# Tile 1's attention heads moved to the plain float32 path, and the weight decodes spread anew

## The chip, the cores and the metric

The kernel runs on one core of one Trainium2 chip. The metric is the device time of one execution in microseconds (us). Three executions of the kernel before gave 879.23, 880.64 and 881.67 us; the median is 880.64 us.

## The reference

Three stages, all in float32 (the four MLP weights of the second and third stage arrive as float64):

```python
# attention: batch 4, 8 heads, 576 positions, head size 64, causal window of 128, ALiBi slopes
scores = (q @ k.T) / 8 - slope[h] * |i - j|          # only where 0 <= i - j < 128
attn = softmax(scores);  x = attn @ v                # x: 2304 tokens x 512
# first MLP: 512 -> 2048 -> 512
x = (s * relu(x @ w_in) ** 2 + b) @ w_out
# second MLP: 512 -> 1024 -> 1024 -> 512
out = (((x @ w1) * (x @ w2)) @ w3) @ w_out2
```

## The kernel before

The 2304 tokens are six tiles of 384. A tile has eight heads in three query blocks of 128; heads are numbered through, g = 8 * tile + head, so tile 0 has g 0 to 7 and tile 1 has g 8 to 15. A query block sees two key blocks of 128, its own and the one ahead of it.

Attention exists in two forms. The **split path** (tiles 1 to 5) cuts each operand into a rounded float32r part and a float32r rest, so that TensorE runs one fast pass per product. Per head: `att_split_q`, `att_split_k` (ScalarE, VectorE, GpSimd), scores in six float32r matmuls (L302, L303, tile `s`), `att_min` on VectorE (L316, L325: both key halves are folded into one of 128 columns, since a query sees at most 128 keys), exp on ScalarE (L339), the division by the sum (`att_norm`, GpSimd L352), three transposes on TensorE (L371, `tp`), a rounded part and a rest (L383, L384, `pp`), two selections on GpSimd that unfold the halves again (L387, `pt`), eight matmuls with V (L424, `pv`), and an addition (L455, L456). The **plain path** (tile 0, `g < EARLY`) does scores in three float32 matmuls on the raw operands (L297), folds nothing, exponentiates 256 columns a block (L333), transposes each key half by itself (L364, `te`), copies (L378, L379, `oe`), multiplies with V that has a column of ones beside it (L404, `xo`), and divides at the end by the sum that this column gave (L436 to L441, `xs`); three more transposes for each pair of heads (L446, `xt`) turn the result.

The first MLP runs 16 chunks for each tile: `mlp_h` (L485 in tile 0, in plain float32; L494 in the others, float32r in three passes) and `mlp_x` (L540, L546, `acc`). Its weights are decoded from float64 beforehand, 32 pieces, each with one operation on ScalarE (L102) and three on VectorE (L104, L107, L113). `tick()` starts one decode and moves those under way by a step.

The order of work: `slot(n, m)` handles one head and, with m, two MLP chunks. Eight slots do tile 0's heads alone; then `"BBBABBABBB"` runs tile 0's MLP in eight slots (B) with the heads 8 to 17 beside it, two of them alone (A); then each slot has a head and two chunks of tiles 1 and up. A scheduler orders the instructions of each engine from a simulated timeline. `tick` is called 1 or 2 times in the head slots (12 in all) and 3 times in each B slot. PSUM has two pools of four banks: `ps_acc`, and `ps_rot` in turn for `s` (two tiles a head), `tp` or `te`, `pv` and `hp`. ScalarE takes its instructions strictly in the order given.

Of the kernel before, what the change touches and what calls it, by code (L numbers as in the profile page):

```python
# [21 lines left out]
P = 128  # L22
TT = 384
# [9 lines left out]
EARLY = H  # L33
# [7 lines left out]
def kernel(  # L41
# [172 lines left out]
    qkraw, vraw, qa, ka, kb, vv, ns, pr, mins, sums, tps, pt, xf, xT, xo = ({} for _ in range(15))  # L214

    def att_load(g):
        if g < NG:
            if g < EARLY and g % 2:
                return
            n = 2 * TT + P + (1 if g < EARLY else 0)  # L220
            raw = ap.tile([P, n], F32, tag="qkraw", name="qkraw", bufs=2)
            nc.sync.dma_start(out=raw, in_=qk0[g // 2] if g < EARLY else qk[g - EARLY])
            if g < EARLY:
                qkraw[g + 1] = raw
            qkraw[g] = raw

    def att_load_v(g):
        if g < NG and g % 2 == 0:
            m = 2 * (D + 1) if g < EARLY else 2 * D
            raw = ap.tile([P, NB + 1, m], F32, tag="vraw", name="vraw", bufs=2)  # L230
            src = v0[g // 2] if g < EARLY else v[(g - EARLY) // 2]
            nc.sync.dma_start(out=raw.rearrange("p n d -> p (n d)"), in_=src)
            vraw[g // 2] = raw

    def att_split_q(g):
        if g < NG:
            sc = -0.125 * 2.0 ** (g % H + 1)
            q_r = qkraw[g][:, :TT]
            if g < EARLY:
                if g % 2 == 0:  # L240
                    a = ap.tile([P, TT], F32, tag="qa", name="qe", bufs=2)
                    nc.scalar.activation(
                        out=a, in_=q_r, func=AF.Identity, scale=qkraw[g][:, -1:]
                    )
                    qa[g] = qa[g + 1] = a
                return
# [8 lines left out]
    def att_split_k(g):  # L255
        if g < NG:
            k_r = qkraw.pop(g)[:, TT:2 * TT + P]
            if g < EARLY:
                ka[g] = k_r
                return  # L260
# [8 lines left out]
    def att_split_v(g):  # L269
# [3 lines left out]
        if g < EARLY:  # L273
# [12 lines left out]
    def att_scores(g):  # L286
# [4 lines left out]
        if g < EARLY:  # L291
            keep_active(s0.rearrange("p n q -> p (n q)"), 2 if g else 10)
        for i in range(NB):
            qs, ks = slice(i * P, (i + 1) * P), slice(i * P, (i + 2) * P)
            if g < EARLY:
                hs, c0 = slice(g % 2 * D, (g % 2 + 1) * D), P if i == 0 else 0
# [9 lines left out]
    def att_min(g):  # L306
        t, h = divmod(g, H)
        dst = ns.pop(g)
        odd = g < EARLY and g % 2
        n = ap.tile([P, NB, 2 * P], F32, tag="vv" if odd else "ns", name="ns")  # L310
        mn = ep.tile([P, NB], F32, tag="mn", name="mn")
        if g >= EARLY:
            e = ap.tile([P, NB, P], F32, tag="pr", name="pr", bufs=2)
        for i in range(NB):
            cs = slice(P if g < EARLY and i == 0 else 0, None)
# [6 lines left out]
        if g < EARLY:  # L322
# [5 lines left out]
    def att_exp(g):  # L328
        e, mn = pr[g], mins.pop(g)
        if g < EARLY:  # L330
            for i in range(NB):
                cs = slice(0 if i else P, None)
# [12 lines left out]
    def att_norm(g):  # L345
        if g < EARLY:
            return
# [9 lines left out]
    def att_transpose(g):  # L357
        e = pr.pop(g)
        if g < EARLY:
# [14 lines left out]
    def att_select(g):  # L374
        tp = tps.pop(g)
        if g < EARLY:
            o = ap.tile([P, 2 * NB, P], F32, tag="pt" if g % 2 else "pp", name="oe")
            nc.scalar.activation(out=o[:, 1:4], in_=tp[0][:, 1:], func=AF.Copy)  # L378
# [14 lines left out]
    def att_v(g):  # L393
        t = g // H
        p, e = divmod(g, 2)
        if g < EARLY:
            o = pt.pop(g)
            if e == 0:
                xo[p] = ps_acc.tile([P, NB, 2, D + 1], F32, tag="acc", name="xo")
            x = vv[p].rearrange("p n (e d) -> p n e d", e=2)  # L400
            for i in range(NB):
                for half in range(2):
                    if i or half:
                        nc.tensor.matmul(  # L404
                            out=xo[p][:, i, e, :], lhsT=o[:, 2 * i + half, :],
                            rhs=x[:, i + half, e, :], start=(half == 0 or i == 0),
# [22 lines left out]
    def att_x(g):  # L429
        t, h = divmod(g, H)  # L430
        p, e = divmod(g, 2)
        if g < EARLY:
            if e:
                acc = xo.pop(p)
                rs = ep.tile([P, NB, 2, 1], F32, tag="sm", name="rs")
# [4 lines left out]
                xs = ap.tile([P, NB, 2, D], F32, tag="cs", name="xs")  # L440
                nc.vector.tensor_tensor(  # L441
                    out=xs, in0=acc[:, :, :, :D], in1=rs.to_broadcast([P, NB, 2, D]), op=ALU.mult
                )
                xf[p] = ps_acc.tile([P, TT], F32, tag="acc", name="xt")
# [13 lines left out]
    def att_xt(g):  # L458
        if g % 2:
            t, h = divmod(g, H)  # L460
            f = xf.pop(g // 2)
            if g < EARLY:
# [499 lines left out]
    def slot(n, m, extra=None):  # L962
# [8 lines left out]
        dec = 2 if mlp and q < NC1 else 1  # L971
# [3 lines left out]
        if s1:  # L975
            splits(n)
            att_scores(n)
            if n + 1 != EARLY:
# [24 lines left out]
        elif n < EARLY:  # L1003
            tick(1 + n % 2)
# [28 lines left out]
        if att:  # L1033
            att_load(n + (2 if n + 2 >= EARLY else 3))
# [4 lines left out]
    for n in range(EARLY):  # L1039
        slot(n, None)  # L1040
    flush(EARLY - 1)
    n, m = EARLY, 0
# [154 lines left out]
```

## Time and profile before

| | |
|---|---|
| median of three runs | 880.64 us |
| the profiled execution, its own time | 882.35 us |
| its span, first to last instruction | 880.6 us |
| TensorE (PE) busy | 857.8 us, 97% of the span |
| VectorE (DVE) busy | 563.5 us, 64% |
| ScalarE (ACT) busy | 485.8 us, 55% |
| GpSimd (POOL) busy | 388.6 us, 44% |
| DMA | 129.57 MB, mean 147 GB/s |

Three stretches matter here: tile 0's heads until 42.27 us, tile 0's MLP with the heads 8 to 16 from there to 143.45 us, and the change to tile 1's MLP until about 164 us. In the timeline each row gives the start, the duration, the engine, the line, the operation, the tile written and those read, and the number of records; a float32 matmul of the program stands as two records. The difference between the starts of two rows is the time that TensorE took for the first of them.

### The profile page before, as it was taken

The numbers are of one execution on the slowest core, as the hardware profiler recorded it, in microseconds if no ns is written. First come the engines' busy times: TensorE is split into PE (matmuls) and PEld (weight loads), VectorE is DVE, ScalarE is ACT, GpSimd is POOL, SyncE is SP. The second block draws the span as 40 slices with busy tenths as digits, with TensorE's granted clock in tenths as the row PEclk, the third lists the DMA queues.
The fourth block names the chain that finished last, engine by engine and source line by source line (L and its number), as shares of the span: only waits on it lengthen the run. The fifth ranks groups of instructions, "written<-read, shape, count | busy, mean of one in ns | idle before, by whom it ended". The sixth has DMA issues, their size and how long they took to land. (4 is left out here: it accounts for less than half of the span.)

```text
span 880.6 us, 13686 instructions
## 1 busy us (share of the span) xinstructions
PE 857.8 (97%) x4676; PEld 777.2 (88%) x4676; DVE 563.5 (64%) x1167; ACT 485.8 (55%) x1140; POOL 388.6 (44%) x419
## 2 busy tenths in 40 slices
PE   8999998999999999999999999999999999999998
PEld 5666666999999999999999999889898889989996
DVE  6888898666878798778863998355434344334233
ACT  6666556777776787777764766344322333222222
POOL 0157666777667676667752302544321233101110
PEclk9999999999999999999999999999999999999999
DMA  8854522112344546445422577824508452530001
GB/s 333 331 200 135 203 84 65 59 55 79 105 147 159 168 168 197 152 168 169 149 96 97 170 260 272 312 84 144 179 28 296 144 183 96 206 117 1 1 1 73
DMA packets 51478, 129.57 MB, mean 147 GB/s; under 512 B 5968, under 2 KB 21328, under 8 KB 51408
## 3 DMA queue, kind: packets, MB, share of 16 engines
q1 hardware_dynamic: 51408, 128.69, 42.6%
q8 instruction: 37, 0.61, 0.3%
q14 instruction: 33, 0.27, 0.1%
HBM read 96.16 MB, written 32.51 MB: 146 GB/s over the span
## 5 line engine op out<-in xcount | busy, mean ns | idle before, releaser
L494 PE MATMUL hp<-x,w 128*128 128x384 f32 x960 | 186.9, 341 | 2.7 <-DVE pp L384 2.5
L494 PEld LDWEIGHTS hp<-x,w 128*128 128x128 f32 x960 | 168.2, 189 | 3.4 <-DVE pp L384 2.7
L546 PE MATMUL acc<-gh,w 128*128 128x384 f32 x640 | 126.3, 339 | 0.8 <-ACT gh L515 0.7
L546 PEld LDWEIGHTS acc<-gh,w 128*128 128x128 f32 x640 | 109.0, 188 | 1.6 <-ACT gh L515 1.4
L815 PE MATMUL d<-xb,wblk 128*128 128x384 f32 x576 | 107.9, 335 | 0.0
L815 PEld LDWEIGHTS d<-xb,wblk 128*128 128x128 f32 x576 | 101.2, 188 | 2.0
L352 POOL TENSOR_SCALAR pr<-pr,sm 128x128 f32<-128x128 f32 x120 | 64.5, 552 | 83.0 <-DVE sm L350 22.7
L913 POOL TENSOR_TENSOR p<-mc 128x384 f32<-128x384 f32 (+2 forms) x30 | 31.3, 1050 | 146.3 <-DVE mc L908 143.9
L815 PE MATMUL u<-xb,wblk 128*128 128x384 f32 x432 | 84.3, 337 | 4.0 <-ACT mc L823 4.0
L387 POOL TENSOR_SCALAR_AFFINE_SELECT pt<-pp 128x768 fp32r<-128x768 f32 x80 | 77.2, 985 | 17.8 <-DVE pp L384 7.9
L854 PE MATMUL oacc<-w3o,ph 128*128 128x512 f32 x270 | 84.8, 395 | 0.0
L815 PEld LDWEIGHTS u<-xb,wblk 128*128 128x128 f32 x432 | 75.2, 188 | 6.8 <-ACT mc L823 6.6
L264 POOL TENSOR_TENSOR kb<-qkraw,ka 128x512 fp32r<-128x512 f32 x40 | 56.6, 1414 | 54.4 <-ACT ka L263 53.9
L904 DVE TENSOR_TENSOR mc<-d,mc 128x384 f32<-128x384 f32 x24 | 13.4, 557 | 94.4 <-PE d L815 94.4
L546 PE MATMUL acc<-gl,w 128*128 128x384 f32 x320 | 69.8, 338 | 2.9 <-DVE gl L523 2.9
L316 DVE CUSTOM_DVE_ANT_0 ns<-s,relm_sb 128x256 f32<-128x256 f32 (+1 forms) x144 | 52.7, 413 | 28.0 <-PE s L303 21.7
L339 ACT ACTIVATE pr<-pr,mn 128x128 f32<-128x128 f32 x120 | 46.9, 392 | 28.0 <-DVE pr L325 27.8
L523 DVE TENSOR_TENSOR gl<-r,gh 128x384 fp32r<-128x384 f32 x80 | 54.2, 678 | 10.4 <-ACT gh L515 9.2
L546 PEld LDWEIGHTS acc<-gl,w 128*128 128x128 f32 x320 | 56.4, 188 | 4.0 <-DVE gl L523 3.9
L854 PEld LDWEIGHTS oacc<-w3o,ph 128*128 128x128 f32 x270 | 50.4, 188 | 10.4
L505 ACT ACTIVATE r<-hp 128x384 f32<-128x384 f32 x96 | 46.4, 484 | 22.1 <-PE hp L494 16.3
L606 POOL TENSOR_TENSOR xs<-xs,xh 128x384 fp32r<-128x384 f32 x28 | 30.1, 1091 | 64.3 <-ACT xh L605 39.4
(120 smaller groups left out, 1683.2 us busy)
## 6 DMA issues: line engine op xcount, KB each, us to landing
qkraw<-qk SPq DMA_DIRECT2D x41, 448.0 KB, 3.3
late<-st SPq DMA_DIRECT2D x23, 512.0 KB, 3.3
w<-late SPq DMA_DIRECT2D x23, 512.0 KB, 6.0
raw<-w_in SPq DMA_DIRECT2D x16, 512.0 KB, 6.1
raw<-w_out SPq DMA_DIRECT2D x16, 512.0 KB, 6.6
wr<-w SPq DMA_DIRECT2D x16, 512.0 KB, 4.7
st<-w3T SPq DMA_DIRECT2D x15, 512.0 KB, 3.7
xs<-x2d SPq DMA_DIRECT2D x32, 192.0 KB, 2.9
```

What stands on the lines that cost most here:

```text
L264: nc.gpsimd.tensor_tensor(out=kl, in0=k_r, in1=k.bitcast(F32), op=ALU.subtract)
L316: nc.vector.tensor_tensor_reduce(out=n[:, i, cs], in0=dst[i][:, cs], in1=relm_sb[:, VARIANT.get(t * NB + i, 0), cs], scale=2.0 ** -(h + 1) ...
L339: nc.scalar.activation(out=e[:, i, :], in_=e[:, i, :], func=AF.Exp, scale=-1.0, bias=mn[:, i:i + 1], accum_out=sm[:, i:i + 1],)
L352: nc.gpsimd.tensor_scalar(out=e[:, i, :], in0=e[:, i, :], scalar1=sm[:, i:i + 1], scalar2=1.0, op0=ALU.mult, op1=ALU.mult,)
L387: nc.gpsimd.affine_select(out=o[:, :, :, e, :], in_=pp.bitcast(F32), pattern=[[0, 2], [0, NB], [sign, P]], compare_op=op, fill=0.0, base=0 ...
L494: nc.tensor.matmul(out=hp, lhsT=wi[c][:, l, k * P:(k + 1) * P], rhs=xT[t, k][:, r, :], start=(n == 0), stop=(n == 3 * KD - 1),)
L505: nc.scalar.activation(out=rt[:, :TT], in_=hps.pop((t, c)), func=AF.Relu)
L523: nc.vector.tensor_tensor(out=gl, in0=rt[:, :TT], in1=gh.bitcast(F32), op=ALU.subtract)
L546: nc.tensor.matmul(out=x2acc[m], lhsT=wo[c][:, l, ms], rhs=g[r], start=(c == 0 and n == 0), stop=(c == NC1 - 1 and n == 2),)
L815: tc.keep_in_program_order(nc.tensor.matmul(out=dst, lhsT=w[:, l, ks], rhs=xblk[bnm, k][:, r, :], start=(start and n == 0), stop=(n == 5), ...
L854: tc.keep_in_program_order(nc.tensor.matmul(out=oacc[t, i], lhsT=p[l][:, cs], rhs=w3o[c][:, r, :], start=(c == 0 and n == 0), stop=(c == N ...
L913: nc.gpsimd.tensor_tensor(out=x, in0=u2[:, n:n + w], in1=m5[:, n:n + w], op=ALU.mult)
```

## The change

`EARLY = H` becomes `PLAIN = 2 * H`: heads 8 to 15 take the plain path too. Places that hold for tile 0 alone now ask `g < H`: the missing first key block, the filling matmuls (`keep_active`), and the pool of `xo` and `xt`. In tile 1 `xo` is a bank of `ps_rot` for each head, `xt` one for each pair, and the rest of the turned result is subtracted on VectorE instead of GpSimd. `tick` now runs once in each head slot (8) and four times in each B slot. q, k and V of tile 1 arrive by pairs of heads, as tile 0's do; the load of head 8 that was issued twice is issued once.

```diff
-EARLY = H
+PLAIN = 2 * H
@@ att_scores
-        if g < EARLY:
+        if g < H:
             keep_active(s0.rearrange("p n q -> p (n q)"), 2 if g else 10)
...
-            if g < EARLY:
-                hs, c0 = slice(g % 2 * D, (g % 2 + 1) * D), P if i == 0 else 0
+            if g < PLAIN:
+                hs, c0 = slice(g % 2 * D, (g % 2 + 1) * D), P if g < H and i == 0 else 0
@@ att_transpose
-                for b in range(max(b0, 1), b0 + n):
+                for b in range(max(b0, int(g < H)), b0 + n):
@@ att_v
-            if e == 0:
+            if g >= H:
+                xo[p] = ps_rot.tile([P, NB, 1, D + 1], F32, tag="rot", name="xo")
+            elif e == 0:
                 xo[p] = ps_acc.tile([P, NB, 2, D + 1], F32, tag="acc", name="xo")
@@ att_x
-                xf[p] = ps_acc.tile([P, TT], F32, tag="acc", name="xt")
+            if e:
+                pool, tag = (ps_acc, "acc") if g < H else (ps_rot, "rot")
+                xf[p] = pool.tile([P, TT], F32, tag=tag, name="xt")
@@ att_xt
-                nc.gpsimd.tensor_tensor(
+                (nc.vector if g < PLAIN else nc.gpsimd).tensor_tensor(
                     out=y[:, 1, :], in0=f, in1=y[:, 0, :].bitcast(F32), op=ALU.subtract
@@ slot
-        dec = 2 if mlp and q < NC1 else 1
+        dec = 3 if mlp and q < NC1 else 1
...
-        elif n < EARLY:
-            tick(1 + n % 2)
+        elif n < H:
+            tick(1)
...
-            att_load(n + (2 if n + 2 >= EARLY else 3))
+            if n + 2 >= PLAIN:
+                att_load(n + 2)
+            elif n % 2 and n + 3 < PLAIN:
+                att_load(n + 3)
```

ScalarE at the end of tile 0's heads, before: the exponentials of heads 6 and 7 are L333, the copies of transposed blocks L378 and L379, a decode's first step L102, the preparation of head 8's operands L248 and L263.

```order
L333 ACTIVATE ns<-ns,mn 128x256
L333 ACTIVATE ns<-ns,mn 128x128
L333 ACTIVATE ns<-ns,mn 128x256
L378 ACTIVATE oe<-te 128x384
L379 ACTIVATE oe<-te 128x256
L102 ACTIVATE z<-raw 128x512
L378 ACTIVATE oe<-te 128x384
L333 ACTIVATE ns<-ns,mn 128x256
L248 ACTIVATE qa<-qkraw 128x384
L263 ACTIVATE ka<-qkraw 128x512
```

The same place now (the copies are L379 and L380):

```order
L333 ACTIVATE ns<-ns,mn 128x128
L333 ACTIVATE ns<-ns,mn 128x256 x2
L333 ACTIVATE ns<-ns,mn 128x128
L333 ACTIVATE ns<-ns,mn 128x256 x2
L379 ACTIVATE oe<-te 128x384
L380 ACTIVATE oe<-te 128x256
L379 ACTIVATE oe<-te 128x384
L380 ACTIVATE oe<-te 128x256
L242 ACTIVATE qe<-qkraw 128x384
```

The decode and the copies that stood between head 7's exponentials now stand elsewhere, and the six exponentials follow one another.

TensorE in the middle of tile 0's MLP, before: a slot with one head (L302, L303 scores, L371 transposes, L424 the product with V) and four chunk steps of `mlp_h` (L485) and `mlp_x` (L540).

```order
L302 MATMUL s_1330<-ka,qa 128x256
L303 MATMUL s_1330<-kb,qa 128x256
L302 MATMUL s_1331<-ka,qa 128x256
L303 MATMUL s_1331<-kb,qa 128x256
L540 MATMUL acc<-r,wz 128x386 x4
L371 MATMUL tp<-ident,pr 128x128 x3
L485 MATMUL hp<-xe,wz 128x384 x4
L424 MATMUL pv<-pt,vv 128x256 x2
L424 MATMUL pv<-pt,vv 128x128 x2
L424 MATMUL pv<-pt,vv 128x256 x2
L424 MATMUL pv<-pt,vv 128x128 x2
L540 MATMUL acc<-r,wz 128x386 x4
```

Such a slot now (L297 scores, L364 transposes, L407 the product with V, L455 the turning of a pair; `mlp_h` is L494 and `mlp_x` L549):

```order
L297 MATMUL s_861<-qkraw,qe 128x256 x2
L297 MATMUL s_862<-qkraw,qe 128x256
L364 MATMUL te<-ident,ns 128x128 x6
L549 MATMUL acc<-r,wz 128x386 x4
L494 MATMUL hp<-xe,wz 128x384 x4
L407 MATMUL xo<-vraw,oe 128x65 x6
L494 MATMUL hp<-xe,wz 128x384 x4
```

Three float32 score matmuls stand where six float32r ones stood, six transposes where three stood, and six products with V where eight stood; the chunk steps around them are the same in number.

## Rows read from the trace of the kernel before

**Rows 1.** Busy time (us), share and instructions of TensorE over the span.

```profile
PE 857.8 (97%) x4676; PEld 777.2 (88%) x4676; DVE 563.5 (64%) x1167; ACT 485.8 (55%) x1140; POOL 388.6 (44%) x419
```

**Rows 2.** Busy time of each engine by stretch, then granted clock, DMA share, GB/s.

```profile
42.27:143.45 101.18, 97.88 (x400) 64.12 (x400) 87.49 (x196) 60.88 (x157) 62.63 (x70) 1.00 0.42 142
164.11:480.00 315.89, 313.66 (x1957) 311.67 (x1957) 237.71 (x499) 229.54 (x568) 213.10 (x242) 1.00 0.40 132
```

**Rows 3.** Timeline of TensorE in tile 0's heads (start, us, line, tile, records).

```profile
13.78 0.77 PE L364 MATMUL te<-ident,ns 128*128 128x128 f32 x5
14.38 0.59 PE L78 MATMUL s<-zeros 128*128 128x512 bf16 x2
...
27.15 1.35 PE L297 MATMUL s<-qkraw,qe 64*128 64x128 f32 x6
28.43 0.77 PE L364 MATMUL te<-ident,ns 128*128 128x128 f32 x5
29.16 0.55 PE L446 MATMUL xt<-ident,xs 128*128 128x128 f32 x3
29.54 1.23 PE L404 MATMUL xo<-vraw,oe 128*128 128x65 f32 x10
30.61 0.59 PE L78 MATMUL s<-zeros 128*128 128x512 bf16 x2
31.13 0.92 PE L297 MATMUL s<-qkraw,qe 64*128 64x128 f32 x4
```

**Rows 4.** Timeline of TensorE in tile 0's MLP, with the split heads.

```profile
53.77 4.68 PE L485 MATMUL hp<-xe,wz 128*128 128x384 f32 x14
58.28 2.76 PE L540 MATMUL acc<-r,wz 128*128 128x386 f32 x8
...
90.42 0.57 PE L302 MATMUL s<-ka,qa 128*128 128x256 f32 x1
90.83 0.28 PE L303 MATMUL s<-kb,qa 128*128 128x256 f32 x1
90.95 0.28 PE L302 MATMUL s<-ka,qa 128*128 128x256 f32 x1
...
100.14 0.58 PE L302 MATMUL s<-ka,qa 128*128 128x256 f32 x1
```

**Rows 5.** Timeline of TensorE, rows with a wait ahead of them (in brackets).

```profile
36.55 0.69 PE L364 MATMUL te<-ident,ns 128*128 128x128 f32 x2 [1.64 <-ACT ns L333]
...
106.35 2.85 PE L485 MATMUL hp<-xe,wz 128*128 128x384 f32 x8 [1.23 <-DVE mn L316]
...
137.54 2.85 PE L485 MATMUL hp<-xe,wz 128*128 128x384 f32 x8 [0.79 <-ACT r L505]
...
155.16 3.49 PE L494 MATMUL hp<-x,w 128*128 128x384 f32 x12 [2.52 <-DVE pp L384]
```

**Rows 6.** Timeline of ScalarE ahead of the wait at 36.55.

```profile
35.05 0.66 ACT L102 ACTIVATE z<-raw 128x512 f32<-128x512 f32 x1
...
35.97 0.52 ACT L333 ACTIVATE ns<-ns,mn 128x256 f32<-128x256 f32 x1
```

**Rows 7.** Stretches of 2 us, columns as in rows 2.

```profile
36.00:38.00 2.00, 1.46 (x4) 1.15 (x5) 1.94 (x5) 1.70 (x5) 0.50 (x1) 0.64 0.98 378
38.00:40.00 2.00, 2.00 (x5) 0.98 (x5) 1.50 (x1) 0.00 (x0) 0.95 (x1) 0.50 1.03 404
...
156.00:158.00 2.00, 2.00 (x8) 2.00 (x7) 0.81 (x1) 1.98 (x5) 2.00 (x4) 0.51 0.01 2
158.00:160.00 2.00, 2.00 (x12) 2.00 (x11) 2.00 (x4) 1.41 (x4) 1.49 (x1) 0.64 0.00 0
```

**Rows 8.** Groups by form, VectorE: 6 to 34 us (first), 43 to 143 us (second).

```profile
L113 DVE SCALAR_TENSOR_TENSOR wz<-raw,z 128x512 uint32<-128x512 uint32 x10 | 6.9, 687 | 0.1
...
L113 DVE SCALAR_TENSOR_TENSOR wz<-raw,z 128x512 uint32<-128x512 uint32 x20 | 18.2, 911 | 0.4
```

**Rows 9.** Groups by form, ScalarE, 6 to 143 us: busy, mean ns, idle before, releasers.

```profile
L102 ACT ACTIVATE z<-raw 128x512 f32<-128x512 f32 x32 | 21.4, 672 | 17.7 <-DVE wz L113 12.8 <-DMA raw<-w_in 4.0 <-DMA raw<-w_out 0.7
```

More of the change, by code (lines that the diff above doesn't have):

```diff
@@ L211, in tick @@
                     flight.remove(x)
-    qkraw, vraw, qa, ka, kb, vv, ns, pr, mins, sums, tps, pt, xf, xT, xo = ({} for _ in range(15))
+    qkraw, vraw, qa, ka, kb, vv, ns, pr, mins, sums, tps, pt, xf, xT, xo, xss = ({} for _ in range(16))
     def att_load(g):
         if g < NG:
-            if g < EARLY and g % 2:
+            if g < PLAIN and g % 2:
                 return
-            n = 2 * TT + P + (1 if g < EARLY else 0)
+            n = 2 * TT + P + (1 if g < PLAIN else 0)
             raw = ap.tile([P, n], F32, tag="qkraw", name="qkraw", bufs=2)
-            nc.sync.dma_start(out=raw, in_=qk0[g // 2] if g < EARLY else qk[g - EARLY])
-            if g < EARLY:
+            nc.sync.dma_start(out=raw, in_=qk0[g // 2] if g < PLAIN else qk[g - PLAIN])
+            if g < PLAIN:
                 qkraw[g + 1] = raw
@@ L402, in att_v @@
                 for half in range(2):
-                    if i or half:
+                    if g >= H or i or half:
                         nc.tensor.matmul(
-                            out=xo[p][:, i, e, :], lhsT=o[:, 2 * i + half, :],
-                            rhs=x[:, i + half, e, :], start=(half == 0 or i == 0),
+                            out=xo[p][:, i, 0 if g >= H else e, :], lhsT=o[:, 2 * i + half, :],
+                            rhs=x[:, i + half, e, :], start=(half == 0 or g < H and i == 0),
                             stop=(half == 1),
@@ L431, in att_x @@
         p, e = divmod(g, 2)
-        if g < EARLY:
-            if e:
+        if g < PLAIN:
+            if e or g >= H:
                 acc = xo.pop(p)
-                rs = ep.tile([P, NB, 2, 1], F32, tag="sm", name="rs")
+                w = 2 if g < H else 1
+                rs = ep.tile([P, NB, w, 1], F32, tag="sm", name="rs")
                 nc.vector.tensor_scalar(
@@ L439, in att_x @@
                 nc.vector.reciprocal(out=rs, in_=rs)
-                xs = ap.tile([P, NB, 2, D], F32, tag="cs", name="xs")
+                if e == 0 or g < H:
+                    xss[p] = ap.tile([P, NB, 2, D], F32, tag="cs", name="xs")
+                xs = xss[p]
                 nc.vector.tensor_tensor(
-                    out=xs, in0=acc[:, :, :, :D], in1=rs.to_broadcast([P, NB, 2, D]), op=ALU.mult
-                )
-                xf[p] = ps_acc.tile([P, TT], F32, tag="acc", name="xt")
+                    out=xs if g < H else xs[:, :, e:e + 1, :], in0=acc[:, :, :, :D],
+                    in1=rs.to_broadcast([P, NB, w, D]), op=ALU.mult,
+                )
+            if e:
+                pool, tag = (ps_acc, "acc") if g < H else (ps_rot, "rot")
+                xf[p] = pool.tile([P, TT], F32, tag=tag, name="xt")
                 for i in range(NB):
@@ L1037, in slot @@
             nc.sync.dma_start(out=relm_sb[:, 2:], in_=relm[:, 2:])
-    for n in range(EARLY):
+    for n in range(H):
         slot(n, None)
-    flush(EARLY - 1)
-    n, m = EARLY, 0
+    flush(H - 1)
+    n, m = H, 0
     pinned[0] = True
```

53 lines of the change are left out of this document (28 added, 25 removed).

## The prediction

> **What bounds the kernel now.** I read the page's busy shares first, then the busy times by stretch, then TensorE's timeline row by row. TensorE is busy for 97% of the span [rows 1]; no other engine comes near it over the whole. The reader should then ask whether a stretch exists where another engine sets the pace. In tile 0's MLP, from 42.27 to 143.45 us, VectorE is busy 87.5 of 101.2 us, which looks like a second bound, but TensorE is busy 97.9 us of the same stretch [rows 2]: all that VectorE, ScalarE and GpSimd cost there shows as 3.3 us of TensorE waiting, in three waits of 1.23, 1.22 and 0.79 us (two of them in [rows 5]). From 164 to 480 us TensorE is busy 313.7 of 315.9 us [rows 2]; the change leaves that stretch alone. So TensorE's own work is the measure, and the other engines' relief is worth no more than the waits that it ends. The waits within reach are these. At the end of tile 0's heads a transpose waits 1.64 us for head 7's last exponential [rows 5], and the granted clock then stands at 0.64 and 0.50 (1.2 GHz for part and all of the two stretches) until 40 us [rows 7]: (1 - 0.64) * 2 + (1 - 0.50) * 2 = 1.7 us, less the idle part, about 1.5 us. In tile 0's MLP there are the 3.3 us. At the change to tile 1's MLP a chunk waits 2.52 us for VectorE's `pp` [rows 5], followed by a clock of 0.51 and 0.64 [rows 7], another 1.6 us or so. Together 3.1 + 3.3 + 4.1 = 10.5 us: the most that the change can give back.
>
> **What a head costs on TensorE, before and after.** This is the main term. Before: from the scores at 90.42 to the next scores at 100.14 lie 9.72 us [rows 4], with 24 float32 records of the MLP in between (eight of `hp`, sixteen of `acc`). A float32 record of 384 columns takes (58.28 - 53.77) / 14 = 0.322 us [rows 4], so the MLP has 7.73 us and the split head 1.99 us.
>
> After: tile 0's heads show the plain path's price. From row to row in [rows 3]: scores 28.43 - 27.15 = 1.28, transposes 0.73, the pair's turning 0.38 (0.19 a head), products with V 1.07; the filling matmuls (0.52) are not in tile 1. Tile 0's heads lack the first key block, tile 1's do not. The sixth block adds two score records of 128 more columns, 2 * 0.107 = 0.21 by the 0.322 us for 384; it takes transposes and products from five to six: 0.88 and 1.28. Sum: 1.49 + 0.88 + 1.28 + 0.19 = 3.84 us, the upper end. For the lower end, five transposes also took 14.38 - 13.78 = 0.60 us [rows 3], so six take 0.72; and a group may open cheaper next to float32 MLP matmuls than among small groups: the split head's first score record holds 0.41 us where the next holds 0.12 [rows 4], and I take these 0.29 us off once. That is 3.39 us. The change costs a head between 1.40 and 1.85 us, eight heads between 11.2 and 14.8 us. I take the middle, 3.62 us a head, **+13.0 us**: neither end is nearer, since tile 1's groups stand partly beside float32 MLP work and partly beside each other. All of it lies on the path, because TensorE has no idle time to put it in.
>
> The Trainium skill bears on this: "TensorE: Matmul & The Clock Gate", section "The mechanism", holds that a weight load runs beside matmuls in flight only where the row group differs. By that each of the twelve records of the product with V would pay load and columns one after the other; with the page's 107 ns a load and 54 ns for 65 columns that is an estimate of 1.93 us where I have 1.28, another 5 us for eight heads. The trace disagrees: ten such records take 1.07 us [rows 3], and from 164 to 480 us loads and matmuls of full height are busy together for 99% of the time [rows 2]. The measurement decides.
>
> **What comes back in tile 0's heads.** Twelve ticks become eight, so four decodes (per decode 0.67 us on ScalarE [rows 9], 0.69 us for L113 [rows 8] and two lighter steps on VectorE) leave this stretch. Up to 31 us nothing is won, since there TensorE paces itself [rows 3] and the loads of the first pieces are issued in the same order. At the end, before, a decode's L102 at 35.05 and copies stood ahead of head 7's last exponential at 35.97 [rows 6], for which TensorE waited until 36.55. Now the six exponentials of heads 6 and 7 follow one another, as the order shows. Then they are ready about when TensorE has done the ten transposes' first eight: the wait of 1.64 us should go, and with it the low clock that came after it. **-3.1 us**; between -3.1 and 0, if another wait takes its place.
>
> **What comes back in tile 0's MLP.** GpSimd loses the k and V splits, the divisions and the selections of eight heads; VectorE loses L325, L249, L384, L349, L350 and L456 for them. It gains four decodes, the division per head (three short operations) and the subtraction for x. L113 takes 911 ns in this stretch and 687 ns while GpSimd is still [rows 8], so each decode also gets shorter. VectorE falls from 87% busy to something near 60%, and is no longer what TensorE waits for. ScalarE is the doubt. Three decodes now start in a row in a B slot, there are only two `z` buffers, and ScalarE takes its queue in order: a third L102 waits for a decode to leave VectorE, and behind it stand relu, exponentials and copies that free PSUM banks. Already L102 spent 12.8 us waiting for L113 [rows 9]. I give back half of the 3.3 us: **-1.6 us**, with 3.3 us gained and 5.3 us lost as ends (below). The moved decodes' loads cost nothing: the stretch uses 0.42 of the DMA engines [rows 2], and the pairwise loads of q and k are half as many. If that cover were gone, decodes would come late and the cost would be as in the third rival.
>
> **What comes back at the change to tile 1's MLP.** Heads 16 and 17 still take the split path there, the same weight splits start there, and now tile 1's last x also comes late, from xo to xt to ScalarE to VectorE, behind these splits. **0 us**, with -4.1 us as an end.
>
> **Sum.** +13.0 - 3.1 - 1.6 = +8.3 us. Against the profiled execution (882.35 us, 1.7 us over the median) that is 890.7 us; against the median 880.64 it is **888.9 us**.
>
> **Rivals.** *All waits go.* With VectorE and GpSimd relieved, all 10.5 us come back and 13.0 - 10.5 = +2.5 us remain: 883.1 us. For it: every wait in [rows 5] leads through ScalarE or VectorE. Against: two of these places keep the split path or gain decodes.
>
> *Faster: the plain groups sink under the MLP.* If weight loads of the transposes and products run wholly under neighbouring float32 matmuls, a head pays columns alone: scores 1.28, transposes 0.32, products 0.65, turning 0.16 (at 0.322 us for 384 columns a record, a transpose one record), 2.4 us, so 0.4 * 8 = +3.3 us, and with all waits gone -7.2 us: 873.4 us. It decides for faster once a plain head costs less than 1.99 + (10.5 - 2.6) / 8 = 2.98 us. Against it: ten product records pace at 0.107 us each in every head of tile 0 that I looked at, with and without small groups beside.
>
> *New waits in the ring of PSUM banks.* A B slot takes six `ps_rot` tiles before (two `hp`, two `s`, `tp`, `pv`) and 7.5 now (two `te`, `xo`, half an `xt`), and each must be emptied by ScalarE or VectorE, whose queues are in order. At one wait of 1.1 us (the mean of the three) in each of eight slots that is 8.6 us, 5.3 us more than now: 13.0 - 3.1 + 5.3 = +15.2 us, 895.8 us. Against: VectorE has room.
>
> **How the numbers follow.** The forecast (884 to 893 us) has 0.56; all waits gone 0.15; plain groups hidden 0.07; new waits 0.22. About 0.3%, 2.6 us, is what a measurement of this kernel can tell from no change. Faster 0.07; same 0.12 (most of the first rival and the low edge of the forecast); slower 0.81. The range leaves out the faster rival and the far end of the third: 881.5 to 896.5 us, where the low end is 11.2 - 10.5 = +0.7 and the high end 14.8 + 1, a few waits beyond.
>
> **What would show it.** In the profile after: a slot's time from scores to scores less its MLP records, 3.4 to 3.8 us a head; no wait ahead of the last transposes of head 7, and a granted clock of 1.00 from 34 to 42 us; TensorE's waits in tile 0's MLP, 3.3 us before, and their releasers; a start of tile 1's MLP about 8 to 10 us later than 143.45. I am wrong if a plain head costs under 3 us, or if waits of over 5 us appear in tile 0's MLP.

## The result and the profile after

The changed kernel took 889.6 us (median of four runs, 887.8 to 897.2) where the kernel before took 880.3 us on the same chip: 9.3 us more, a ratio of 1.012 with a 95% interval of 1.007 to 1.017. The forecast was 888.9 us. Some executions of several kernels here are 1.5% or more longer at a lower granted clock; the medians contain them, the ratios leave them out. The profiled execution of the changed kernel took 889.65 us, its span is 887.9 us, against 882.35 and 880.6 before; that is 2.0 us over the median for the kernel before and at the median for the changed one.

The page gives TensorE 12.2 us more and every other engine less than in [rows 1]:

```profile
PE 870.0 (98%) x4742; PEld 786.0 (89%) x4744; DVE 537.7 (61%) x1147; ACT 478.4 (54%) x1100; POOL 333.7 (38%) x359
```

By stretch (the columns of [rows 2]; the first row is tile 0's MLP until the first chunk of tile 1's, the second a later stretch as long as that of [rows 2]):

```profile
39.94:157.83 117.89, 115.70 (x481) 74.97 (x481) 72.80 (x194) 62.22 (x133) 18.79 (x19) 1.00 0.38 133
172.99:488.90 315.91, 314.58 (x1966) 312.91 (x1965) 239.78 (x499) 229.12 (x571) 212.19 (x241) 1.00 0.39 132
```

VectorE fell to 72.8 of 117.9 us (62%) and GpSimd to 18.8, so the relief came as the diff says. TensorE was idle for 2.2 us in the first row. The long stretch of 315.9 us is as full as it was.

TensorE's timeline at the end of tile 0's heads:

```profile
34.87 1.26 PE L364 MATMUL te<-ident,ns 128*128 128x128 f32 x10
36.01 1.56 PE L494 MATMUL hp<-xe,wz 128*128 128x384 f32 x4
37.40 0.49 PE L455 MATMUL xt<-ident,xs 128*128 128x128 f32 x3
37.73 1.23 PE L407 MATMUL xo<-vraw,oe 128*128 128x65 f32 x10
38.88 1.13 PE L297 MATMUL s<-qkraw,qe 64*128 64x256 f32 x4
39.94 1.33 PE L407 MATMUL xo<-vraw,oe 128*128 128x65 f32 x10
41.20 0.70 PE L297 MATMUL s<-qkraw,qe 64*128 64x256 f32 x2
```

The wait of 1.64 us ahead of the last transposes [rows 5] is gone. The granted clock from 34 to 42 us is 1.00, where [rows 7] has 0.64 and 0.50. The same work (four `hp` records, the turning, twenty `xo` records) is done at 41.20 - 1.06 (the scores at 38.88) = 40.14 us; before, it was done at 42.27, the start in [rows 2]. That is 2.1 us earlier.

But 15 us ahead of that a low clock appeared that was not there before. In stretches of 2 us, columns as in [rows 7]:

```profile
20.00:22.00 2.00, 2.00 (x10) 1.64 (x9) 2.00 (x9) 1.80 (x4) 0.00 (x0) 0.69 1.05 392
22.00:24.00 2.00, 2.00 (x12) 2.00 (x11) 1.32 (x3) 2.00 (x6) 0.00 (x0) 0.50 0.67 264
24.00:26.00 2.00, 2.00 (x12) 1.32 (x11) 0.19 (x1) 0.28 (x1) 0.00 (x0) 0.96 0.09 31
```

It costs 0.31 * 2 + 0.50 * 2 + 0.04 * 2 = 1.7 us.

A slot of tile 0's MLP with a plain head, and the turning of a pair:

```profile
86.51 1.56 PE L297 MATMUL s<-qkraw,qe 64*128 64x256 f32 x6
88.00 0.87 PE L364 MATMUL te<-ident,ns 128*128 128x128 f32 x6
88.71 2.76 PE L549 MATMUL acc<-r,wz 128*128 128x386 f32 x8
91.30 2.74 PE L494 MATMUL hp<-xe,wz 128*128 128x384 f32 x8
93.88 1.45 PE L407 MATMUL xo<-vraw,oe 128*128 128x65 f32 x12
95.17 2.80 PE L494 MATMUL hp<-xe,wz 128*128 128x384 f32 x8
97.90 1.34 PE L297 MATMUL s<-qkraw,qe 64*128 64x256 f32 x5
...
157.59 0.49 PE L455 MATMUL xt<-ident,xs 128*128 128x128 f32 x3
157.83 0.77 PE L503 MATMUL hp<-x,w 128*128 128x384 f32 x3
```

From start to start: scores 1.49, transposes 0.71, products with V 1.29, turning 0.24 a pair here. From scores to scores lie 11.39 us with 24 records of the MLP; at 0.322 us each [rows 4] these are 7.73 us and the head 3.66, with half a turning 3.8.

All waits of TensorE between 42 and 165 us:

```profile
48.54 0.70 PE L297 MATMUL s<-qkraw,qe 64*128 64x256 f32 x2 [0.39 <-DVE mn L316]
83.45 0.55 PE L455 MATMUL xt<-ident,xs 128*128 128x128 f32 x3 [0.86 <-DVE xs L447]
110.36 2.86 PE L549 MATMUL acc<-r,wz 128*128 128x386 f32 x8 [0.94 <-ACT r L519]
160.55 2.00 PE L503 MATMUL hp<-x,w 128*128 128x384 f32 x9 [1.24 <-ACT x L476]
```

Three of 2.2 us together stand where three of 3.3 us stood [rows 5], and one of 1.24 us, for tile 1's last x, where 2.52 us and a low clock stood [rows 5, 7]. The wait of 0.94 us for L519 comes from a load: ahead of L519 in ScalarE's queue stands the preparation of a split head, and this waits 1.98 us for the head's q and k.

```profile
108.75 0.63 ACT L263 ACTIVATE ka<-qkraw 128x512 fp32r<-128x512 f32 x1 [1.98 <-DMA qkraw<-qk]
```

Tile 1's MLP starts at 157.83 us, 14.4 us later than before and not 8 to 10. Its start was a poor mark: eight records of tile 0's last `acc` stood behind it before (from 144.98 to 147.63 us) and stand ahead of it now. Its first product with the second weight (`acc<-gh`) starts at 159.62 us before and at 168.34 now, 8.7 us later.

A span is TensorE's busy time and its idle time. Where the granted clock is low, busy time holds a part that is no work: (1 - clock) * 2 summed over the 2-us stretches below 1.00 in tile 0's heads and MLP and at the change, less what of them is idle. Taking that off leaves the work, and the kernels can be set beside each other:

| kernel | time | span | busy | idle | low clock | work |
|---|---|---|---|---|---|---|
| before | 880.3 | 880.6 | 857.8 | 22.8 | 3.2 | 854.6 |
| after | 889.6 | 887.9 | 870.0 | 17.9 | 1.7 | 868.3 |
| before, decodes spread as after | 886.1 | 884.3 | 858.2 | 26.1 | 3 | 855 |
| after, decodes spread as before | 886.7 | 884.6 | 868.3 | 16.3 | 0 | 868.3 |
| half of tile 1's heads plain, new spread | 892.3 | 889.6 | 863.9 | 25.7 | 0 | 863.9 |
| half plain, old spread | 895.1 | 892.7 | 865.9 | 26.8 | 3 | 863 |
| before with filler on TensorE | 891.6 | 889.5 | 871.0 | 18.5 | 3.1 | 867.9 |
| before, VectorE relieved (low bits) | 870.4 | 870.4 | 853.0 | 17.4 | 0 | 853.0 |
| the same with filler | 885.8 | 884.0 | 867.0 | 17.0 | 0 | 867.0 |

In the kernel with filler the granted clock stands at 1.00 in every stretch up to the last matmul, but its first rows run at nearly half speed. The first and the third group of scores, in the kernel before and then in that one:

```profile
5.76 1.38 PE L297 MATMUL s<-qkraw,qe 64*128 64x128 f32 x6
12.50 1.35 PE L297 MATMUL s<-qkraw,qe 64*128 64x128 f32 x6
```

```profile
5.75 2.50 PE L304 MATMUL s<-qkraw,qe 64*128 64x128 f32 x6
15.04 1.35 PE L304 MATMUL s<-qkraw,qe 64*128 64x128 f32 x6
```

The third group starts 2.54 us later, and 0.61 us of waits between the two are gone, so 3.1 us of busy time are no work; they stand in the table as low clock. In the changed kernel the first group takes 1.92 us instead of 1.31; these 0.6 us are not taken off.

So the change is +13.7 us of work, -4.9 us of idle time and -1.5 us of low clock: +7.3 us of span. The work of kernels with the same matmuls differs by up to 2 us in the table (853.0 to 855), so that a difference of 1 us there says nothing.

### The profile page after: what moved, and what is told of

It reads as the page before. It is cut to its first block, busy times and chain, and to the rows that moved or that the text cites. A ratio compares the mean times of both kernels' runs of the same rounds, so it can differ in the third digit from the quotient of the medians.

```text
span 887.9 us, 13643 instructions
## 1 busy us (share of the span) xinstructions
PE 870.0 (98%) x4742; PEld 786.0 (89%) x4744; DVE 537.7 (61%) x1147; ACT 478.4 (54%) x1100; POOL 333.7 (38%) x359
## 4 chain that ended last, share of the span: by engine, by line
PE 81%; DVE 4%; DMA 4%; ACT 4%; issue 3%; POOL 3%; SPq 0%; DVEq 0%; ACTq 0%; POOLq 0%
PE hp L503 16%; PE acc L555 16%; PE oacc L863 10%; PE d L824 9%; PE u L824 7%; PE w3a L590 5%; PE hp L494 4%; PE acc L549 3%; PE pv L427 2%; PE s L297 2%; PE xo L407 2%; DMA xs<-x2d 1%; PE s L302 1%; PE s L303 1%; PE tp L371 1%
## 5 line engine op out<-in xcount | busy, mean ns | idle before, releaser
L264 POOL TENSOR_TENSOR kb<-qkraw,ka 128x512 fp32r<-128x512 f32 x32 | 44.4, 1389 | 145.8 <-ACT ka L263 120.4
L352 POOL TENSOR_SCALAR pr<-pr,sm 128x128 f32<-128x128 f32 x96 | 49.1, 526 | 67.6 <-ACT z L150 24.9
L388 POOL TENSOR_SCALAR_AFFINE_SELECT pt<-pp 128x768 fp32r<-128x768 f32 x64 | 59.8, 955 | 7.6 <-PE pv L427 6.1
L863 PE MATMUL oacc<-w3o,pl 128*128 128x512 f32 x135 | 53.4, 395 | 0.0
```

The source lines that it names most:

```text
L264: nc.gpsimd.tensor_tensor(out=kl, in0=k_r, in1=k.bitcast(F32), op=ALU.subtract)
L352: nc.gpsimd.tensor_scalar(out=e[:, i, :], in0=e[:, i, :], scalar1=sm[:, i:i + 1], scalar2=1.0, op0=ALU.mult, op1=ALU.mult,)
L388: nc.gpsimd.affine_select(out=o[:, :, :, e, :], in_=pp.bitcast(F32), pattern=[[0, 2], [0, NB], [sign, P]], compare_op=op, fill=0.0, base=0 ...
L863: tc.keep_in_program_order(nc.tensor.matmul(out=oacc[t, i], lhsT=p[l][:, cs], rhs=w3o[c][:, r, :], start=(c == 0 and n == 0), stop=(c == N ...
```

## The experiments

Each ran beside the kernel before on the same chip, and ratios are against those runs. Rounded times of the kernel before were 880.5, 879.9, 881.4 and 881.9 us in the four groups of runs.

### The spread of the decodes alone, and the plain path alone

The kernel before with the new numbers of decodes, and the changed kernel with the old ones:

```diff
-        dec = 2 if mlp and q < NC1 else 1
+        dec = 3 if mlp and q < NC1 else 1
...
-            tick(1 + n % 2)
+            tick(1)
```

> The kernel before with only the decodes moved: one tick in each of tile 0's head slots (8 in place of 12), four in each MLP slot of tile 0; tile 1's heads stay on the split path. Theory (TensorE's own work for eight plain heads is the loss, the moved decodes bring back the wait at the end of tile 0's heads): 877.5 to 880.5 us, no wait of TensorE ahead of head 7's last transposes. Rival (the loss sits in the moved decodes, four in an MLP slot holding up ScalarE's queue): 883 us or more, with waits of TensorE in tile 0's MLP above the 3.3 us of before.

> The changed kernel with the decodes where they were: twelve ticks among tile 0's heads, three in each MLP slot. Theory (plain heads' own TensorE work): 888 to 893 us, as the changed kernel or up to 3 us more. Rival (the moved decodes are the loss): 879 to 884 us.

The spread alone took 886.1 us, ratio 1.007 (1.005 to 1.009). The theory, which was the prediction's, expected a gain of 0 to 3 us and got a loss of 5.7; the time is the rival's. The wait at the end of tile 0's heads is still there (1.13 us where 1.64 stood), and beside the split heads the wait of 1.22 us for GpSimd's division (L352) grows to 3.19 us; all in all TensorE idles 6.8 us in tile 0's MLP, where 3.3 us stood. TensorE's timeline, then ScalarE's and VectorE's ahead of it, in that kernel:

```profile
34.78 1.24 PE L364 MATMUL te<-ident,ns 128*128 128x128 f32 x5 [1.13 <-ACT ns L333]
...
114.07 0.78 PE L371 MATMUL tp<-ident,pr 128*128 128x128 f32 x2 [3.19 <-POOL pr L352]
```

```profile
108.71 0.68 ACT L102 ACTIVATE z<-raw 128x512 f32<-128x512 f32 x1 [1.77 <-DVE wz L113]
109.89 0.40 ACT L339 ACTIVATE pr<-pr,mn 128x128 f32<-128x128 f32 x1 [0.50 <-DVE pr L325]
```

```profile
106.93 1.15 DVE L104 TENSOR_SCALAR z<-z 128x512 uint32<-128x512 uint32 x1
109.30 0.56 DVE L325 TENSOR_TENSOR pr<-ns 128x384 f32<-128x384 f32 x1
110.95 1.24 DVE L113 SCALAR_TENSOR_TENSOR wz<-raw,z 128x512 uint32<-128x512 uint32 x1
113.32 0.15 DVE L350 RECIPROCAL sm<-sm 128x3 f32<-128x3 f32 x1
```

A decode's first step (L102) stands in ScalarE's queue for 1.77 us until an earlier decode leaves VectorE. But it is done at 109.39 us, and the exponentials behind it still wait for the folding (L325), which VectorE does only at 109.30, behind a decode's steps. The exponentials end at 111.15 us; the reciprocal (L350) that the division needs comes at 113.32, behind another decode's L113. So what holds TensorE here is VectorE's queue with the decodes in it, more than ScalarE's order, which the rival blamed and the prediction doubted.

The plain path with the old spread took 886.7 us, ratio 1.008 (1.006 to 1.010): between the two expectations. Its only waits between 33 and 175 us, in TensorE's timeline:

```profile
35.06 0.44 PE L364 MATMUL te<-ident,ns 128*128 128x128 f32 x2 [0.70 <-ACT ns L333]
82.00 0.55 PE L455 MATMUL xt<-ident,xs 128*128 128x128 f32 x3 [0.86 <-DVE xs L447]
108.95 2.86 PE L549 MATMUL acc<-r,wz 128*128 128x386 f32 x8 [0.98 <-ACT r L519]
```

Its work is the same 868.3 us as the changed kernel's. So the plain path costs about 6 us, and the new spread up to 3 us on top: 1.6 us of idle time and 1.7 us of low clock in the table. The intervals of the two ratios overlap, and the low clock does not come with every execution: the one execution of the changed kernel with a mean granted clock of 1.000 has a span of 886.0 us, two of the plain path with the old spread 884.2 and 884.6 us. That leaves about 1.6 us for the spread, which the times alone do not show.

### Work on TensorE without any relief

The kernel before with sixteen bf16 matmuls ahead of the scores of each of heads 8 to 15, into a bank that the scores overwrite:

```diff
+FILL = 16
...
+        if EARLY <= g < 2 * H:
+            fill = ident.bitcast(BF16)
+            for _ in range(FILL):
+                nc.tensor.matmul(
+                    out=dst[0], lhsT=fill[:, :P], rhs=fill, start=True, stop=True
+                )
```

> The kernel before with TensorE work that nobody uses added to each head of tile 1: sixteen matmuls of 128x256 in bfloat16 into the bank that the scores then overwrite, 128 in all, some 0.11 to 0.13 us each, 14 to 16.6 us together, about what eight plain heads cost more. Nothing is taken from the other engines. Theory (what came back came from the relief of VectorE and GpSimd): the waits of before stay, 893 to 897 us. Rival (a slower TensorE alone lets the other engines catch up, so the same waits vanish without relief): 886 to 891 us.

891.6 us, ratio 1.015 (1.012 to 1.018): 11.1 us for 13.3 us of work (867.9 - 854.6; from row to row the 128 matmuls take as much), inside neither range but nearer the rival. TensorE's waits from 33 to 175 us (L371 is `te` here, L501 `hp`, L391 `pp`):

```profile
38.88 0.44 PE L371 MATMUL te<-ident,ns 128*128 128x128 f32 x2 [1.63 <-ACT ns L340]
165.63 2.38 PE L501 MATMUL hp<-x,w 128*128 128x384 f32 x12 [2.49 <-DVE pp L391]
```

The three waits of tile 0's MLP, 3.3 us, have vanished although no other engine was given any relief: there a slower TensorE alone lets the others catch up. It does so nowhere else: the waits at the end of tile 0's heads and at the change to tile 1's MLP stand as they did (1.64 and 2.52 us before). Idle time fell by 4.3 us in all, and the 3.1 us of low clock at the start are as much as the 3.2 us before. The 4.9 us of the changed kernel are made up in another way: 1.6 us at the end of tile 0's heads, 1.1 us in its MLP, 1.3 us at the change, the rest in small pieces.

### Half of the heads

`PLAIN = H + 4`: heads 8 to 11 plain, 12 to 15 split, with the new spread and with the old; q, k and V of each head are laid out for its path on the host.

> The changed kernel with four of tile 1's heads (8 to 11) on the plain path and four (12 to 15) on the split path; ticks as in the changed kernel. Theory (a price per head, 1.9 us of TensorE each, 7.6 us for four, less the wait at the end of tile 0's heads and half of the later ones): 883 to 887 us. Rival (one place, such as the change to tile 1's MLP, carries the whole loss): near 880 or near 889 us.

> Heads 8 to 11 on the plain path, 12 to 15 split, and the decodes spread as before (12 among tile 0's heads, 2 in a slot of its MLP). Of the runs so far: all eight heads plain with the old spread 886.7 us, none of them plain 880.5; four heads plain with the new spread 892.3, with 9.5 us more of TensorE busy than before and no fewer waits. Theory A (the plain path costs about 0.75 us a head net of the waits that it removes, and the new spread costs 3 to 6 us wherever split heads are still beside it): 882.5 to 885.5. Theory B (four heads of each kind in turn is itself bad, since the split heads come when the queues are behind): 888 to 891, near the 892.3 of the new spread.

892.3 us (ratio 1.015, 1.013 to 1.017) and 895.1 us (1.017, 1.015 to 1.019): both are slower than either pure version. The first is above both of its expected times; the second is above theory B's range, and theory A fell, since the old spread didn't help. TensorE's timeline in the first, then in the second, where the first split heads come up beside the MLP:

```profile
117.28 2.86 PE L549 MATMUL acc<-r,wz 128*128 128x386 f32 x8 [2.62 <-ACT r L519]
119.97 0.27 PE L371 MATMUL tp<-ident,pr 128*128 128x128 f32 x1
```

```profile
117.27 4.55 PE L549 MATMUL acc<-r,wz 128*128 128x386 f32 x8 [2.63 <-ACT r L519]
121.66 0.27 PE L371 MATMUL tp<-ident,pr 128*128 128x128 f32 x1
```

In both, ScalarE waits 2.27 us for L325, the folding on VectorE that only split heads have, and the square of the MLP chunk (L519) that TensorE waits for stands behind the exponentials. The work went up by 8 to 9 us, where four heads should have cost about 7 us by the full count, and idle time went up from 22.8 to 25.7 and 26.8 us. But the heads that differ are not where all of this lies. From tile 1's first `acc<-gh` to the end the kernels do the same; the kernel before, the changed one, and the two with half of the heads:

```profile
159.62:880.60 720.98, 709.12 (x4008) 675.66 (x4006) 432.68 (x852) 382.74 (x888) 309.00 (x327) 1.00 0.41 138
168.34:887.90 719.56, 708.31 (x4010) 676.15 (x4008) 433.73 (x850) 381.52 (x886) 309.09 (x329) 1.00 0.40 138
164.74:889.60 724.86, 710.02 (x4008) 675.64 (x4006) 431.70 (x853) 382.00 (x890) 308.61 (x328) 1.00 0.40 137
167.06:892.70 725.64, 709.37 (x4008) 675.82 (x4006) 434.40 (x852) 381.94 (x888) 307.05 (x327) 1.00 0.40 137
```

There the two lose 3.9 and 4.7 us against the kernel before, most of it as idle time (14.8 and 16.3 us, for 11.9 us). Up to there they are 5.1 and 7.4 us behind it (3.2 us of the 7.4 are low clock), and the changed kernel is 8.7 us behind. So it is not shown that mixing the two kinds of head is bad in itself; why the later stretch is longer was not found out.

### What ended the wait in tile 0's heads

```diff
-            tick(1 + n % 2)
+            tick(2)
```

> The kernel before with one edit: 2 decodes in each of tile 0's eight head slots (16, not 12), so that fewer are left for its MLP slots (16, not 20). The opposite step of the run that moved four the other way and came out at 886.1. Theory (a decode in an MLP slot stands in ScalarE's and VectorE's queues ahead of what TensorE waits for there): 876 to 879.5, with fewer waits of TensorE between 42 and 160 us. Rival (tile 0's heads run at 0.96 of DMA and end with a wait of 1.6 us, so that more decodes there lengthen them by as much): 880 to 884.

882.7 us, ratio 1.003 (1.001 to 1.005), so theory failed here too: four decodes fewer in the MLP, and not faster. The time is in the rival's range, but not for its reason: the first chunk of tile 0's MLP starts at 36.35 us, where it started at 37.02. The wait at 36 us fell to 0.54 us, but head 8's scores waited 1.57 us for `vv` at 42.92 and a transpose 1.68 us for `pr` at 114.64.

```diff
-            att_load(n + (2 if n + 2 >= EARLY else 3))
+            if n != EARLY - 2:
+                att_load(n + (2 if n + 2 >= EARLY else 3))
```

> The kernel before loads head 8's q and k twice (after heads 5 and 6). Here the second load is left out, which the change does too. 128 x 896 x 4 bytes = 0.46 MB, 1.2 us at the 367 GB/s of tile 0's heads. Theory (the wait of 1.6 us ahead of head 7's transposes is on VectorE's and ScalarE's queues, and no transfer ends last): 880 to 881.5. Rival (the load holds up raw weights, whose decodes hold up the copies of head 7): 876.5 to 879, and the wait at 34.9 us shorter than 0.8.

880.7 us, ratio 1.001 (0.999 to 1.003), and the wait still 1.43 us. The second load of head 8 costs nothing that can be measured here.

### Relief of VectorE without work on TensorE

The kernel before, without one of the three steps of VectorE in the 20 decodes beside tile 0's MLP; first the sign step:

```diff
-            pin(nc.vector.scalar_tensor_tensor(
-                out=zu, in0=wu[:, :, 1], scalar=0x80000000, in1=zu,
-                op0=ALU.bitwise_and, op1=ALU.bitwise_or,
-            ))
+            if not (plain and pinned[0]):
+                pin(nc.vector.scalar_tensor_tensor(
+                    out=zu, in0=wu[:, :, 1], scalar=0x80000000, in1=zu,
+                    op0=ALU.bitwise_and, op1=ALU.bitwise_or,
+                ))
```

> The kernel before without one of VectorE's three steps of a decode (the sign bit of the weight) in the 20 decodes beside tile 0's MLP: 20 x 0.69 us = 13.8 us of VectorE's 100.7 there, and nothing else. The weights lose their sign, so the times alone count. It gives relief to VectorE without the plain path's work on TensorE. Theory (the 2.5 us at the change to tile 1's MLP, the 3.4 us of half clock behind it and most of the 3.3 us inside tile 0's MLP come from VectorE's backlog): 880.5 - 4 to - 7 = 873.5 to 876.5. Rival (they come from ScalarE's order or the ring of PSUM banks, and VectorE is not late): 878.5 to 881.

869.3 us, ratio 0.988 (0.986 to 0.990): 10.6 us, more than the theory asked. VectorE was relieved of more than 13.8 us: in the trace the step stands in 12 of 33 decodes, so 21 lost it and not 20, and VectorE is busy for 546.8 us where it was for 563.5, 16.7 us less. To rule out that one step's place in the order, or weights without a sign, the last step went instead, and the sign step wrote the plain tile:

> The kernel before, in which the 20 decodes beside tile 0's MLP leave out VectorE's last step instead of the sign step: the three low bits of the float32 mantissa are dropped (a weight is then short by up to one part in 2^20), and the sign step writes the plain tile itself. 20 x 0.69 to 0.91 us = 14 to 18 us of VectorE. It asks whether the 10.6 us come from VectorE's load and not from that one step or from weights without a sign. Theory (load): 867.5 to 872. Rival (the sign step's place in the order): 876 to 881.

870.4 us, ratio 0.988 (0.984 to 0.992), with 14.5 us less of VectorE (563.5 - 549.0). So it is the load, and not the one step. Load is not all: the kernel with more decodes among tile 0's heads had 6.4 us less of VectorE between 42 and 160 us (94.2 for 100.7) and won nothing. The scheduler orders other instructions anew when a step is missing (without the sign step, ScalarE's order differs from about its 80th row on), so that the edit is not a removal alone. The page of the version without the low bits, TensorE's waits in it from 34 to 175 us, and two stretches of 2 us (its line numbers are a few higher: L368 is `te`, L489 `hp`):

```profile
PE 853.0 (98%) x4676; PEld 774.6 (89%) x4676; DVE 549.0 (63%) x1146; ACT 485.9 (56%) x1140; POOL 384.6 (44%) x419
```

```profile
36.59 0.44 PE L368 MATMUL te<-ident,ns 128*128 128x128 f32 x2 [1.63 <-ACT ns L337]
47.66 2.20 PE L489 MATMUL hp<-xe,wz 128*128 128x384 f32 x6 [0.76 <-ACT xe L468]
```

```profile
36.00:38.00 2.00, 1.41 (x6) 0.99 (x7) 1.85 (x4) 1.75 (x5) 0.45 (x1) 1.00 1.02 405
38.00:40.00 2.00, 2.00 (x19) 1.84 (x17) 0.00 (x0) 0.69 (x2) 1.01 (x1) 1.00 1.04 415
```

The waits at 106 to 138 us and at the change are gone (0.76 us at 47.66 is new), idle time falls by 5.4 us, the low clock by 3.2 and the work by 1.6. Not all of it is relief: the low clock at 36 to 40 us, 1.5 us, stayed away behind a wait that is as long as before (1.63 us), and the 1.6 us of work, with the same matmuls, were not explained. This version beats both kernels and keeps the signs of the weights, at the price of 21 pieces that are short by up to one part in 2^20.

The same relief in the changed kernel (the sign step; 25 decodes by the trace):

> The changed kernel without the sign step of its 24 decodes beside tile 0's MLP (24 x 0.69 = 16.6 us of VectorE; the weights lose their sign, so the times alone count). The same edit took 10.6 us off the kernel before. Theory (with the plain heads TensorE itself sets the pace of tile 0's MLP, VectorE is not late any more, and relief buys only what is left of waits and half clock there, 2.2 + 1.2 + 1.7 us at most): 885 to 889. Rival (VectorE still sets the pace behind TensorE's modelled busy time, and relief is worth as much as before): 877 to 881.

889.9 us, ratio 1.010 (1.007 to 1.013), against 889.6 us: nothing. That is above the whole of the theory's range, on its side of the rival's. What took 10.6 us off the kernel before takes none off the changed one. The waits that are left there (2.2 us in tile 0's MLP, 1.2 us at the change) are not won back by this relief; one of them is for a load of q and k, as shown above.

And the filler in the version without the low bits:

> The run without the low bits (870.4 us) and, on top of it, the filler of the earlier run: 16 bf16 matmuls ahead of the scores of each of heads 8 to 15, which added 16.6 us of TensorE's work to the kernel before and 11.2 us to its time. Theory (relief of VectorE and a slower TensorE take away the same waits, so that they don't add up): with the waits of tile 0's MLP gone already, the filler costs all of its length, 870.4 + 15.5 to 17 = 886 to 887.5. Rival (each takes away waits of its own): 870.4 + 11 = 881.5 or less.

885.8 us, 15.3 us more than without filler (14.7 us if each is set against the runs of the kernel before beside it), where the same matmuls cost the kernel before 11.1 us. That is 0.2 us under the theory's range and far from the rival's. The spans say the same: +13.6 us for 14.0 us of work. So the filler pays nothing back once VectorE is relieved, and about 4 us without that: relief and a slower TensorE take away the same waits, those of tile 0's MLP.

### TensorE's work taken back

```diff
-                    if g >= H or i or half:
+                    if g >= H and half or g < H and (i or half):
...
-                            rhs=x[:, i + half, e, :], start=(half == 0 or g < H and i == 0),
+                            rhs=x[:, i + half, e, :], start=(half == 0 or g >= H or i == 0),
```

> The changed kernel with half of the products with V of tile 1's heads left out (the key half ahead of the query block: 3 of 6 matmuls, 6 of 12 records a head; heads 8 to 15 are then not the reference's). 8 heads x 6 records x 0.107 us = 5.1 us of TensorE, nothing of the other engines. Theory (the plain path's cost is TensorE's work at its full length): 889.6 - 5.1 = 884.5, between 883.5 and 885.5. Rival (as with the filler in the kernel before, a faster TensorE meets the others' waits again, and about half comes back): 886.5 to 888.5.

886.6 us, ratio 1.006 (1.002 to 1.009), 882.2 to 903.6 us over its runs: by the medians 3.0 us less than the changed kernel, 4.1 us less against the runs beside each (+5.3 and +9.3 us). Its trace has a span of 884.3 us (-3.6), busy 866.0 us with 1.7 us of low clock, so 864.3 us of work (-4.0), and 18.3 us idle (+0.4). The time lies between the two expectations, at the rival's edge, and decides nothing by itself; by the trace the 48 records were worth 4.0 us rather than 5.1, 0.083 us each. As waits little came back in sum, but for two reasons that cancel: TensorE idles 1.4 us more in tile 0's MLP and 1.1 us less at the change.

## Why the prediction was right, step by step

**The sum** for the profiled execution was 882.35 + 8.3 = 890.7 us; it took 889.65. Term by term the traces give +13.7 - 2.1 - 1.1 - 2.9 = +7.6 us (the spans +7.3). That the forecast came within 1 us is luck: three terms came out 0.5 to 1.0 us dearer than taken, and one 2.9 us cheaper.

**The head.** 3.62 us was taken, 3.39 to 3.84 allowed; by its parts and by the period it came to 3.6 to 3.8. The term of +13.0 us is +13.7 by the table, 0.6 of it the slow first rows. Scores (1.49) and products (1.28 to 1.29) came as worked out; transposes were cheaper (0.71 for 0.88), and the MLP groups beside them a little dearer. Twelve product records took 1.29 us and not the 1.93 us of the estimate beside the Trainium skill's "TensorE: Matmul & The Clock Gate" (section "The mechanism"), so that the trace disagrees with the rule here too. The same section also lets a load into the background weight buffer go ahead of matmuls in flight, which would fit the trace; no run here tells the two apart.

**Tile 0's heads**, -3.1 us: -2.1 us at the end of the stretch, which the new low clock at 20 to 26 us has already made smaller by its 1.7 us. The effect was right, the cause was not. The prediction put it on the four decodes moved away; with these moved alone the wait stays at 1.13 us, with four more decodes put there instead it falls to 0.54 us, and with the plain path and the old spread to 0.70 us. It ends only where the new spread and plain heads come together. That the plain path does its part there is in keeping with head 8, whose split (L248, L263 in the order of before) no longer stands in ScalarE's queue; this was not tried by itself.

**Tile 0's MLP**, -1.6 us: 3.3 us of waits became 2.2, -1.1 us. The last of them is for L519 on ScalarE, the engine that was doubted, but ScalarE waits there for a load of q and k and not for a decode. That loads cost nothing, as the prediction had it, is true of the weights' loads alone.

**The change to tile 1's MLP**, 0 us: here a term was mis-sized. x did come late, as it said, and TensorE waits 1.24 us for it, but this takes the place of 2.52 us and 1.6 us of low clock: -2.9 us. The far end of -4.1 us was nearer than 0.

**The steps that failed** are this term and the cost of the decodes. Moving four decodes was taken as a gain at the end of tile 0's heads and as no loss beside its MLP; alone it costs the kernel before 5.7 us, and in the changed kernel 1.6 us of idle time, about 3 us with the low clock of that one execution. It was hidden in the sum because the change to tile 1's MLP gave back 2.9 us.

**What relief is worth.** The prediction held that it is worth no more than the waits that it ends, and named 10.5 us as the most. Relieving VectorE alone (14.5 and 16.7 us of it) took 10.9 and 10.6 us off. The size agrees, in part by luck: of the 10.2 us between the spans, 5.4 are idle time and 1.7 the low clock behind the wait for `pp`; the other 3.1 us are not shown to be relief. What the prediction had too low is the share that comes back at the change. Which waits go with what is shown by the runs: those of tile 0's MLP go with relief of VectorE or with a slower TensorE, that at the change with relief but not with the slower TensorE (2.49 us there), and that at the end of tile 0's heads with neither (1.63 us in both).

**The rivals.** All waits go: 883.1 us was too low by 6.5 us. Most of the old waits did go and relieving VectorE more buys nothing (889.9 us), but 3.4 us of waits stand in tile 0's MLP and at the change, a low clock of 1.7 us came, and the eight heads cost 0.7 us more. Plain groups hidden under the MLP: no, a head costs 3.7 us. New waits in the ring of PSUM banks: not with all heads plain (2.2 us); where plain and split heads meet, 2.6 us a time, but through L325 and ScalarE's order, not through the ring.

**Readings that were off**, without weight in the sum. In the rival of hidden groups six transposes of one record each are 6 * 0.107 = 0.64 us and not 0.32, so that its time is 876 us and not 873.4. Loads and matmuls that are busy for 311.7 and 313.7 of 315.9 us are busy together for at least 98% of them. Of VectorE's two other steps of a decode only L104 is lighter than L113 while GpSimd is still (421 ns; L107 takes 689). And up to 31 us TensorE does wait once, 1.38 us for `qe`; the change left that at 1.24 us.

## What to carry to other kernels

Where one engine is busy for 97% of a stretch and another for 86%, the second can still cost time, there and in the stretch behind it, and only relief without new work on the first shows how much (here 10.6 us). Work added to the busiest engine ends some of the others' waits by itself (here three, 3.3 us), so that those must not be counted again as a gain of the relief that comes with it. A change that makes two edits can hide one's loss behind the other's gain: the plain path costs about 6 us, the decodes 1.6 to 3.

## What was not expected of the hardware

The granted clock can fall or stay after the same wait. In the two kernels with half of the heads plain, TensorE's rows are equal to 0.02 us from 79 us up to a wait of 2.62 and 2.63 us at 117.3 us. Behind it, in a stretch of 2 us, first the new spread, then the old:

```profile
118.00:120.00 2.00, 2.00 (x8) 1.12 (x7) 1.00 (x3) 0.94 (x3) 2.00 (x6) 1.00 0.22 34
```

```profile
118.00:120.00 2.00, 2.00 (x5) 1.10 (x4) 1.00 (x3) 0.93 (x3) 2.00 (x6) 0.55 0.28 27
```

Eight records of the MLP take 2.7 us (117.28 to 119.97) at 2.4 GHz in the one and 4.4 us (117.27 to 121.66) mostly at 1.2 GHz in the other. In the same way the wait of 1.63 us at 36.59 us left the clock at 1.00 in the kernel without low bits, where one of 1.64 us at 36.55 was followed by 0.64 and 0.50 before [rows 5, 7], and the changed kernel's low clock at 20 us follows a wait of 1.24 us for `qe` where the kernel before has 1.38 us and no low clock. It differs between executions of one kernel too: the four of the changed kernel have mean granted clocks of 0.994 to 1.000. And the start of the kernel with filler shows rows at nearly half speed where the profile's clock says 1.00, so the rows themselves are the better witness. A term for a low clock behind a wait is therefore a chance, of 0 to 3.2 us a kernel in the table, and not a sum.
